# Second product of units 4 to 17 by seven block products alone, with forms made in fp32; the order of all work as one list

## The chip, the cores and the metric

The kernel runs on one NeuronCore of a Trainium2 chip. The metric is device time in microseconds (us) of one execution. The engines are TensorE (PE; PEld is its weight load), VectorE (DVE), ScalarE (ACT), GpSimd (POOL) and SyncE (SP), which issues most DMAs. Each engine works through its own list of instructions in order; semaphores hold one back until what it needs is done.

## The reference

```python
# q, k, v: (8, 8, 576, 64), phi: (8, 8, 576, 32), w_in: (512, 2048), w_out: (2048, 512)
a = softmax over the sequence of phi                      # 32 memory slots
k_m = einsum('bhsm,bhsd->bhmd', a, k);  v_m = the same with v
attn = softmax(q @ k_m.T / sqrt(64))
x = (attn @ v_m), heads side by side: 4608 tokens x 512
h = x @ w_in
g = h - tanh(h)
return g @ w_out                                          # 4608 x 512
```

The weights arrive as 64-bit floats.

## The kernel before

**Numbers.** Factors of the large products are pairs of fp16 tiles, high part and low part (`ah`/`al`, `win_hi`/`win_lo`, `wout_hi`/`wout_lo`, `gg[:, 0]`/`gg[:, 1]`). A product is the sum of high by high, high by low and low by high, all into fp32 PSUM. The 64-bit weights are turned into fp32 by three integer operations on DVE (`to_f32`), rounded to fp16 on ACT (`conv`), and their low halves formed on DVE, POOL or PE (`low`, `low_pool`, `low_pe`).

**Tiling.** The 4608 tokens are 18 units of 256, the 2048 hidden features four groups `fb` of 512; a unit and a group make a block, 72 blocks in all. For each of the 8 batches the attention gives `ah`/`al`, and `att_p` multiplies the memory's values with `w_in`, so that the first product `mm1` (word `H`) goes straight from attention weights to hidden values `hp` in PSUM.

**A block.** `mm1` ends with the square of `hp` on ACT (`uu`). The cubic for h - tanh(h) is `g1` on DVE (L576, one PSUM and one SBUF tile in), `g1_square` on ACT (L581), `g2` on DVE (L586, two SBUF tiles in from unit 4 on), giving the fp32 tile `h3` of 128 x 1024. `g2_high` rounds it to fp16 on ACT (L592), `g3` subtracts on POOL for the low part (L597). The second product adds the block into the unit's sums `o0` and `o1` (128 tokens x 512 each), in PSUM until the unit's last block.

**The second product.** In units 0 to 3 it is plain, `mm2` (L640). From unit 4 on it is `mm2_blocks`: the high by high part is plain, 8 matmuls of 512 columns (`main`, L697); the two cross terms go by seven products of blocks in place of eight (a scheme of Strassen's kind), 7 x 4 matmuls of 256 columns (L704). The seven need sums and differences ("forms") of four blocks of `g`, made by `a_forms` on DVE (L610) from the fp16 halves, and forms of `w_out`, made once from its fp16 halves by `b_form` (L622). Four of the seven add up in a PSUM tile `x` shared by all units; `evict` (L757 to L769) joins `x` with `o0`, `o1` on DVE and sends the unit out.

**The order.** Up to the third block of unit 4 it is the word list `START`, one word a step of one piece of work (`H10` the first product of unit 1, group 0; `T` and `L` weight conversion; `Z` a pair of filler matmuls). From there a loop over blocks writes the rest by the tables `PLAN`, `PLAN3`, `PLAN_C`: first product, `g1`, the square, `a_forms` of the block before, `g2`, the second product of two blocks back, rounding, `g3`. `in_order` fixes each engine's order as written.

```python
        g1(u, fb)
        do(0)
        g1_square(u, fb)
        a_forms(*forms.pop())
        g2(u, fb)
        queue.append((u, fb))
        v, vb = queue.pop(0)
        mm2_blocks(v, vb, vb == 0, vb == NFB - 1)
        do(1)
        g2_high(u, fb)
        g3(u, fb, nc.gpsimd)
```

Of the kernel before, what the change touches and what calls it, by code (L numbers as in the profile page):

```python
# [1138 lines left out]
```

## Time and profile before

| | |
|---|---|
| median of 3 runs | 663.79 us (661.35 to 664.32) |
| the profiled execution | 663.12 us, its span 661.3 us |
| mean granted TensorE clock | 0.997 |
| POOL, low part of `g` (L597) | 67 of 2.17 us |
| DVE, forms of `g` (L610) | 224, 0.43 to 0.49 us mean |
| DVE, cubic (L576, L586) | 144 of 1.22 us |

A profile row of a group reads: line, engine, operation, out<-in by the program's names, shapes, count | busy us, mean ns of one | idle time of that engine just before them, and what ended it. A row of waits reads: who <- what it waited for: us in total, times, longest. A timeline row reads: start, length, engine, what it was.

### The profile page before, as it was taken

The page shows a single profiled execution, that of the slowest core. Times are in us where ns is not written, and L with a number is a line of the kernel's source. Part 1 is how long each engine was busy: PE and PEld are TensorE (multiplying, and loading weights), DVE is VectorE, ACT ScalarE, POOL GpSimd, SP SyncE. Part 2 cuts the span into 40 slices and gives each one's busy share as a digit, 9 for nine tenths or more (in the row PEclk, how much of TensorE's full clock was granted, in tenths as well). Part 3 has the DMA queues.
Part 4 walks back from the last instruction along what each step waited for, and adds up shares of the span by engine and source line. Part 5 has one row for each costly group of instructions (what it writes and reads, how often), then busy time and mean ns, then how long its engine had stood idle before and what let it go on. Part 6 is the DMA issues. An engine that isn't in the chain of part 4 may idle for free.

```text
span 661.3 us, 15304 instructions
## 1 busy us (share of the span) xinstructions
PE 635.6 (96%) x6562; PEld 452.1 (68%) x6562; DVE 539.1 (82%) x840; ACT 352.1 (53%) x445; POOL 222.7 (34%) x141
## 2 busy tenths in 40 slices
PE   8678999999999999999999999999999999899996
PEld 4254656555657777777777777777786767677885
DVE  6798999999846797875888789778977897979573
ACT  4576576665523555545555555555555546554441
POOL 0224331443112234451435243633362423332321
PEclk9998999999999999999999999999999999999999
DMA  8999253333122301324231433143314432224101
GB/s 341 400 361 384 64 196 105 126 99 113 65 96 101 135 30 73 113 100 145 93 113 66 167 105 113 66 168 103 115 47 152 140 119 65 97 96 160 34 33 37
DMA packets 25995, 84.96 MB, mean 128 GB/s; under 512 B 2880, under 2 KB 2880, under 8 KB 25152
## 3 DMA queue, kind: packets, MB, share of 16 engines
q1 hardware_dynamic: 24624, 81.55, 34.7%
q10 hardware_dynamic: 1296, 2.36, 0.9%
q8 instruction: 53, 0.87, 0.5%
q14 instruction: 22, 0.18, 0.1%
HBM read 72.37 MB, written 11.53 MB: 127 GB/s over the span
## 4 chain that ended last, share of the span: by engine, by line
PE 61%; DVE 23%; DMA 5%; issue 4%; ACT 4%; POOL 2%; SPq 0%; DVEq 0%; ACTq 0%; POOLq 0%
PE hs L561 16%; PE x L704 11%; PE o L697 11%; PE o L704 8%; PE o L640 5%; DMA raw<-in_w_out_dram 3%; DVE h L586 3%; DVE h L576 3%; PE h L561 2%; DVE f L610 2%; DVE wt L387 2%; PE pp L513 2%; DVE ph L531 2%; PE pkv L223 2%; PE o1h L640 2%
## 5 line engine op out<-in xcount | busy, mean ns | idle before, releaser
L597 POOL TENSOR_TENSOR g<-h,g 128x1024 f16<-128x1024 f32 x67 | 145.7, 2174 | 357.1 <-ACT g L592 294.3
L561 PEld LDWEIGHTS <-ph 128*128 128x128 f16 x2304 | 177.7, 98 | 22.2 <-issue 6.6
L561 PE MATMUL hs<-ah,ph 128*128 128x256 f16 (+3 forms) x1152 | 151.5, 246 | 0.0
L592 ACT ACTIVATE g<-h 128x1024 f16<-128x1024 f32 x72 | 76.0, 1056 | 113.5 <-DVE h L586 105.0
L576 DVE SCALAR_TENSOR_TENSOR h<-hs,u 128x1024 f32<-128x1024 f32 x54 | 65.7, 1217 | 77.2 <-ACT u L568 76.9
L561 PE MATMUL hs<-al,ph 128*128 128x256 f16 (+3 forms) x576 | 127.6, 246 | 0.3 <-POOL al L504 0.3
L581 ACT ACTIVATE u<-u,beta 128x1024 f32<-128x1024 f32 x72 | 82.5, 1148 | 61.0 <-DVE h L576 60.6
L697 PE MATMUL o<-wout_hi,g 128*128 128x512 f16 x432 | 104.7, 379 | 2.3 <-DVE r L769 2.3
L704 PEld LDWEIGHTS <-f 128*128 128x128 f16 x896 | 87.7, 98 | 10.2
L586 DVE SCALAR_TENSOR_TENSOR h<-u,h 128x1024 f32<-128x1024 f32 x72 | 87.6, 1216 | 0.7 <-ACT u L581 0.7
L568 ACT ACTIVATE u<-hs 128x1024 f32<-128x1024 f32 x54 | 55.0, 1019 | 59.4 <-PE hs L561 55.3
L704 PEld LDWEIGHTS <-g 128*128 128x128 f16 x672 | 64.2, 98 | 28.7 <-issue 7.3
L704 PE MATMUL x<-bt,f 128*128 128x256 f16 x672 | 82.5, 273 | 0.0
L697 PEld LDWEIGHTS <-g 128*128 128x128 f16 x432 | 40.6, 98 | 46.5 <-issue 10.8
L640 PEld LDWEIGHTS <-g 128*128 128x128 f16 x384 | 36.7, 98 | 46.6 <-issue 4.3
L640 PE MATMUL o<-wout_hi,g 128*128 128x512 f16 x192 | 59.0, 379 | 0.0
L610 DVE TENSOR_TENSOR f<-g 128x512 f16<-128x512 f16 x112 | 50.7, 493 | 4.0 <-POOL g L597 3.4
L561 PE MATMUL h<-ah,ph 128*128 128x256 f16 (+3 forms) x384 | 50.7, 248 | 1.1 <-DVE h L576 1.1
L561 PE MATMUL h<-al,ph 128*128 128x256 f16 (+2 forms) x192 | 42.9, 248 | 0.1
L531 DVE SCALAR_TENSOR_TENSOR ph<-pp,ph 128x1024 f16<-128x1024 f32 x31 | 37.7, 1215 | 0.7 <-ACT ph L526 0.3
L526 ACT ACTIVATE ph<-pp 128x1024 f16<-128x1024 f32 x32 | 32.5, 1017 | 7.6 <-PE pp L513 7.5
L640 PE MATMUL o<-wout_lo,g 128*128 128x512 f16 x96 | 36.4, 379 | 0.0
(146 smaller groups left out, 934.2 us busy)
## 6 DMA issues: line engine op xcount, KB each, us to landing
kv<-in_kva_dram SPq DMA_DIRECT2D x20, 516.0 KB, 3.9
q<-in_qt_dram SPq DMA_DIRECT2D x16, 576.0 KB, 4.2
chk<-in_w_in_dram SPq DMA_DIRECT2D x16, 512.0 KB, 5.2
chk<-in_w_out_dram SPq DMA_DIRECT2D x16, 512.0 KB, 3.7
out_dram<-r SPq DMA_DIRECT2D x27, 256.0 KB, 2.3
kv<-in_kva_dram SPq DMA_DIRECT2D x6, 1032.0 KB, 9.7
raws<-in_w_in_dram SPq DMA_DIRECT2D x12, 512.0 KB, 8.0
raw<-in_w_out_dram SPq DMA_DIRECT2D x12, 512.0 KB, 8.9
```

The source lines that it names most:

```text
L531: nc.vector.scalar_tensor_tensor(pl, pa, S_P / (S_V * S_W), ph, op0=ALU.mult, op1=ALU.subtract)
L561: nc.tensor.matmul(hp[:, k, tu : tu + w], px[:, g, cs], d[ax][:, g, ta : ta + w], start=(n == 0), stop=(n == 5),)
L568: nc.scalar.activation(uu, hp, AF.Square, scale=1.0 / (S_A * S_P))
L576: nc.vector.scalar_tensor_tensor(h3, hp, C2 * S_G / (S_A * S_P), uu, op0=ALU.mult, op1=ALU.mult)
L581: nc.scalar.activation(uu, uu, AF.Square, bias=c["beta"])
L586: nc.vector.scalar_tensor_tensor(h3, uu, CC, hp, op0=ALU.add, op1=ALU.mult)
L592: nc.scalar.activation(gg[:, 0], h3, AF.Copy)
L597: eng.tensor_tensor(gg[:, 1], h3, gg[:, 0], op=ALU.subtract)
L610: nc.vector.tensor_tensor(o, x, y, op=op)
L640: nc.tensor.matmul(o, gx[:, k, P * tt : P * tt + P], wx[:, 4 * fb + k, :], start=(first and k == 0 and wx is wout_hi and gx is gh), stop=( ...
L697: nc.tensor.matmul(o[th], gg[:, 0, k, P * th : P * th + P], wout_hi[:, 4 * fb + k, :], start=(first and k == 0), stop=False)
L704: nc.tensor.matmul(dst, a(1 - n, kk), b(n, kk), start=(new and kk == 0 and n == 0), stop=(end and kk == 1 and n == 1))
```

## The change

1. In units 4 to 17 the plain part is gone: each of the seven products has all three terms, 7 x 6 matmuls of 256 columns (`mm2_blocks`).
2. The forms of `g` are made from the fp32 tile `h3` (`s_forms`, four DVE operations on 128 x 256 fp32) and then split: the high half by one ACT operation of 128 x 1024, the low half by one POOL operation of 128 x 1024 (`s_high`).
3. Of `g` itself three of its four blocks are split, by two ACT and two POOL operations (512 and 256 elements; `a_high`, `a_low`).
4. The forms of `w_out` are made from an fp32 sum of its halves and split in the same way (`b_sum`, `b_form` on DVE, `b_high` on ACT, `b_low` on POOL), per group.
5. The weight conversion works on 1024 elements where it worked on two times 512; pairs of raw weight blocks come in one DMA.
6. `START`, the tables and the loop are replaced by one list, `ORDER`, in which a word stands once for each step of its piece; a second product has three to five steps, an eviction six. The DMA scratch is 1024 bytes.

```diff
+ORDER = """
+i3:pp5 i1:gg i0:gg T0 T0 FX0 Z0.0 Z0.0 Z0.0 Z0.0 X0 T0 i6:kv3 T3 T3 T3 i4:kv2 Z0.0 Z0.0 Z0.0 Z0.0 Z0.0 Z0.0 Z0.0 Z0.0 Z0.0 Z0.0 Z0.0 T2 T2 Z0.0 T2
...
-        for r, t in zip(r32, ts):
-            nc.vector.scalar_tensor_tensor(
-                t, r[:, :, 0], 29, t, op0=ALU.logical_shift_right, op1=ALU.bitwise_or
-            )
+        for low, high, t in parts:
+            nc.vector.scalar_tensor_tensor(t, low, 29, t, op0=ALU.logical_shift_right, op1=ALU.bitwise_or)
...
-        eng.tensor_tensor(gg[:, 1], h3, gg[:, 0], op=ALU.subtract)
+    def a_parts(u, fb):
+
+        h3, gg = hs[u, fb], gs[u, fb]
+        if (u, fb) not in SEVEN:
+            return ((h3, [gg[:, n] for n in range(2)]),)
+        return (
+            (h3[:, 2:4], [gg[:, n, 2:4] for n in range(2)]),
+            (a_block(h3, 0, 0), [a_block(gg[:, n], 0, 0) for n in range(2)]),
+        )
+
+    def a_high(u, fb):
+        gs[u, fb] = big.tile([P, 2, 4, UT], F16, tag="gg", name=f"g{u}{fb}", bufs=3)
+        for x, (hi, _) in a_parts(u, fb):
+            nc.scalar.activation(hi, x, AF.Copy)
+
+    def a_low(u, fb, eng):
+        for x, (hi, lo) in a_parts(u, fb):
+            eng.tensor_tensor(lo, x, hi, op=ALU.subtract)
...
-        gg = gs[u, fb][1]
-        a11, a21, a12, a22 = (a_block(gg, th, kh) for kh in range(2) for th in range(2))
-        f = big.tile([P, 2, 4, 2, P], F16, tag="uu", name=f"f{u}{fb}")
-        s4, s3, s1, s2 = (f[:, :, i] for i in range(4))
+        h3 = hs[u, fb]
+        a11, a21, a12, a22 = (a_block(h3, th, kh) for kh in range(2) for th in range(2))
+        s = big.tile([P, 4, 2, P], F32, tag="ss", name=f"s{u}{fb}")
+        s1, s2, s3, s4 = (s[:, i] for i in range(4))
         for o, x, y, op in ((s3, a21, a11, ALU.subtract), (s1, a21, a22, ALU.add), (s2, s3, a22, ALU.add), (s4, a12, s2, ALU.subtract)):
             nc.vector.tensor_tensor(o, x, y, op=op)
+    def s_high(u, fb):
+
+        s = fs[u, fb]
+        f = big.tile([P, 2, 4, 2, P], F16, tag="uu", name=f"f{u}{fb}")
+        nc.scalar.activation(f[:, 0], s, AF.Copy)
+        yield
+        nc.gpsimd.tensor_tensor(f[:, 1], s, f[:, 0], op=ALU.subtract)
+        fs[u, fb] = f
...
+    def b_sum(fb):
+
+        bts["w", fb] = b = big.tile([P, 4, 512], F32, tag="bw", name=f"bw{fb}", bufs=1)
+        ks = slice(4 * fb, 4 * fb + 4)
+        nc.vector.tensor_tensor(b, wout_hi[:, ks], wout_lo[:, ks], op=ALU.add)
+
+    def b_form(fb):
+
+        b = bts["w", fb]
+        b11, b12, b21, b22 = (b[:, 2 * kh : 2 * kh + 2, 256 * nh : 256 * nh + 256] for kh in range(2) for nh in range(2))
+        for o, x, y in ((b11, b12, b11), (b12, b12, b22), (b22, b22, b11), (b21, b21, b22)):
+            nc.vector.tensor_tensor(o, x, y, op=ALU.subtract)
...
         def prod(dst, a, b, new=False, end=False):
             for kk in range(2):
-                for n in range(2):
+                for na, nb in ((0, 0), (0, 1), (1, 0)):
                     nc.tensor.matmul(
-                        dst, a(1 - n, kk), b(n, kk), start=(new and kk == 0 and n == 0), stop=(end and kk == 1 and n == 1)
+                        dst, a(na, kk), b(nb, kk), start=(new and kk == 0 and na == 0 and nb == 0), stop=(end and kk == 1 and na == 1)
                     )
...
+        prod(x[:, 0, hi], af(1), bf(0, 0), new=xfirst)
+        prod(x[:, 0, lo], ab(0, 0), bb(0, 0), end=xlast)
+        yield
+        prod(x[:, 1, lo], af(2), bf(1, 1), new=xfirst)
+        prod(x[:, 1, hi], af(3), bf(0, 1), end=xlast)
...
+        prod(o[0][:, hi], af(4), bb(1, 1), new=first)
+        prod(o[0][:, lo], ab(0, 1), bb(1, 0), end=last)
+        yield
+        prod(o[1][:, lo], ab(1, 1), bf(1, 0), new=first, end=last)
```

Three places show what this makes of the engines' lists. The first is PE inside a second product of the steady part before: the end of the plain part on a tile `g` (both factors high), and the first cross products.

```order
L697 LDWEIGHTS g_4330
L697 MATMUL o_4281<-wout_hi,g_4330 128x512
L704 LDWEIGHTS g_4330
L704 MATMUL o_4280<-wout_hi,g_4330 128x256
L704 LDWEIGHTS g_4330
L704 MATMUL o_4280<-wout_lo,g_4330 128x256
```

And after, inside a second product: the end of the product of a form `f` with a form `bt` of the weights, and the start of the next, on `g` and `w_out` themselves.

```order
L761 LDWEIGHTS f_5365
L761 MATMUL x<-bt_2221,f_5365 128x256
L761 LDWEIGHTS g_5495
L761 MATMUL x<-wout_hi,g_5495 128x256
L761 LDWEIGHTS g_5495
L761 MATMUL x<-wout_lo,g_5495 128x256
```

No matmul of 512 columns is left in these units; all are of 256, each with a weight load of its own.

The second place is DVE in the steady part before: the cubic's two steps (`h`) with the forms `f` of the block before between them.

```order
L576 SCALAR_TENSOR_TENSOR h_3568<-hs,u_3566 128x1024
L610 TENSOR_TENSOR f_3573<-g_3515 128x2x256 x2
L610 TENSOR_TENSOR f_3573<-f_3573,g_3515 128x2x256
L610 TENSOR_TENSOR f_3573<-g_3515,f_3573 128x2x256
L586 SCALAR_TENSOR_TENSOR h_3568<-u_3566,h_3568 128x1024
```

After, in a like stretch (`s` are the fp32 forms, L630 and L642 the cubic's steps):

```order
L367 RECIPROCAL sz_4263<-sz_4263 128x18
L630 SCALAR_TENSOR_TENSOR h_4268<-hs,u_4261 128x1024
L642 SCALAR_TENSOR_TENSOR h_4268<-u_4261,h_4268 128x1024
L675 TENSOR_TENSOR s_4296<-h_4176 128x256 x2
L675 TENSOR_TENSOR s_4296<-s_4296,h_4176 128x256
L675 TENSOR_TENSOR s_4296<-h_4176,s_4296 128x256
L675 TENSOR_TENSOR s_4301<-h_4268 128x256 x2
```

The forms have moved from between the two steps to behind them, and the forms of two blocks can follow each other; what stands between the two steps differs from block to block.

The third place is POOL before: one low part of `g` a block, with the softmax steps (`sc`) and the low part of the attention weights (`al`) between.

```order
L597 TENSOR_TENSOR g_4016<-h_3958,g_4016 128x1024
L305 TENSOR_TENSOR sc_3969<-sc_3969,sm_4024 128x576
L597 TENSOR_TENSOR g_4111<-h_4053,g_4111 128x1024
L318 TENSOR_TENSOR sc_3969<-sc_3969,sz_4116 128x576
L597 TENSOR_TENSOR g_4206<-h_4147,g_4206 128x1024
```

After:

```order
L684 TENSOR_TENSOR f_4173<-s_4002,f_4173 128x1024
L356 TENSOR_TENSOR sc_3974<-sc_3974,sm_4090 128x576
L684 TENSOR_TENSOR f_4240<-s_4120,f_4240 128x1024
L666 TENSOR_TENSOR g_4125<-h_4092,g_4125 128x512
L666 TENSOR_TENSOR g_4125<-h_4092,g_4125 128x2x128
L369 TENSOR_TENSOR sc_3974<-sc_3974,sz_4263 128x576
```

A block now has three operations on POOL, the forms' low half and two of `g`.

More of the change, by code (lines that the diff above doesn't have):

```diff
@@ new lines, in b_low, with segment, sums @@
+    def b_low(fb):
+        for k in range(0, 4, 2):
+            ks = slice(k, k + 2)
+            nc.gpsimd.tensor_tensor(bts[fb][:, 1, ks], bts["w", fb][:, ks], bts[fb][:, 0, ks], op=ALU.subtract)
+    acc = {}
+    def segment(u, fb):
+        part = [f for f in ((0, 1), (2, 3)) if fb in f][0] if u in SPLIT else tuple(range(NFB))
+        return part, [f for f in part if (u, f) in SEVEN]
+    def sums(u):
+        acc[u] = [ps_o.tile([P, DM], F32, tag=f"o{i}", name=f"o{u}{i}") for i in range(2)]
@@ L628, in mm2 @@
+    def mm2(u, fb):
+        if (u, fb) in SEVEN:
+            yield from mm2_blocks(u, fb)
+            return
+        part, seven = segment(u, fb)
+        first, last = fb == part[0], fb == part[-1]
+        gg = gs[u, fb]
         gh, gl = gg[:, 0], gg[:, 1]
@@ L632, in mm2 @@
         elif first:
-            acc[u] = [ps_o.tile([P, DM], F32, tag=f"o{i}", name=f"o{u}{fb}{i}") for i in range(2)]
+            sums(u)
         both, less = ((wout_hi, gh), (wout_lo, gh)), ((wout_hi, gl),)
         order = [(0, both), (0, less), (1, both), (1, less)] if last else [(0, both), (1, both), (0, less), (1, less)]
-        for tt, part in order:
+        for n, (tt, terms) in enumerate(order):
+            if n == 2:
+                yield
             o = acc[u][tt]
             for k in range(4):
-                for wx, gx in part:
+                for wx, gx in terms:
                     nc.tensor.matmul(
@@ L815, in split_path, with go @@
+        "T": conv, "L": low_pool, "Lv": low, "Lp": low_pe,
+        "BS": b_sum, "BF": b_form, "BH": b_high, "BL": b_low,
+        "SI": squares_in, "NI": norms_in, "SO": squares_out, "NO": norms_out, "SS": squares_sum, "CW": window,
+        "GG": lambda: check(tc, c, big), "GX": lambda: check_all(tc, c, ps_a), "XX": steady, "WD": flag,
+        "M": mm2, "E": evict, "R": load_part, "OP": save_part, "O": save,
     }
     going = {}
-    def go(word, whole=True):
-        name = word.rstrip("0123456789")
-        run = going.pop(word, None) or STEPS[name](*(int(x) for x in word[len(name):]))
-        if run is None or not hasattr(run, "send"):
+    def go(word):
+        if ":" in word:
+            k, tag = word.split(":")
+            n = int(k[1:])
+            if k[0] == "k":
+                load_raw(n, tag, "chk")
+            elif tag in PAIRS:
+                load_raws(n + 16 * (k[0] == "o"), tag)
+            else:
+                load_raw(n + 16 * (k[0] == "o"), tag)
@@ L917, in split_path @@
-    a_forms(*forms.pop())
-    for u, fb in queue:
-        mm2_blocks(u, fb, fb == 0, fb == NFB - 1)
-    c["wide"] = nc.values_load(c["bad"][0:1, 0:1], min_val=0, max_val=1)
-    evict()
+    for word in ORDER.split():
+        go(word)
     in_order(tc, c["first"])
@@ L1000, in wide_path @@
         att.top_all(b, d)
-        list(att.expo(b, d))
+        att.expo(b, d)
+        att.expo_exp(b, d)
         att.pool(b, d)
```

464 lines of the change are left out of this document (200 added, 264 removed), and 12 rows, old and new, of tables (PLAN, PLAN3, PLAN_C).

## The prediction

> **What bounds the kernel now.** I read the page first, then busy time by stretches, the waits, the timeline of one steady block and the groups by form.
>
> ```profile
> span 661.3 us, 15304 instructions
> PE 635.6 (96%) x6562; PEld 452.1 (68%) x6562; DVE 539.1 (82%) x840; ACT 352.1 (53%) x445; POOL 222.7 (34%) x141
> ```
>
> The profiled execution took 663.1 us, 0.7 under the median of the runs (663.8); 1.8 us lie outside its span. PE is busy for 96%, but the stages differ:
>
> ```profile
> core 0: us, PE busy (x) PEld busy (x) DVE busy (x) ACT busy (x) POOL busy (x), PEclk, DMA share, GB/s
> 0.00:20.00 20.00, 17.12 (x92) 7.91 (x92) 15.00 (x30) 9.81 (x16) 0.95 (x10) 1.00 0.92 354
> 20.00:40.00 20.00, 14.06 (x195) 6.51 (x196) 14.93 (x32) 10.72 (x20) 7.63 (x7) 1.00 0.97 377
> 40.00:60.00 20.00, 15.77 (x205) 11.53 (x204) 18.78 (x30) 15.90 (x27) 3.19 (x3) 0.91 1.00 397
> 100.00:120.00 20.00, 20.00 (x227) 11.66 (x226) 19.93 (x32) 13.28 (x22) 4.42 (x3) 1.00 0.46 162
> 180.00:200.00 20.00, 20.00 (x157) 11.21 (x156) 10.57 (x15) 4.26 (x5) 3.47 (x2) 1.00 0.24 80
> 260.00:320.00 60.00, 59.69 (x622) 45.69 (x621) 44.59 (x73) 30.71 (x39) 22.17 (x13) 1.00 0.31 104
> 380.00:440.00 60.00, 60.00 (x701) 45.55 (x700) 50.22 (x80) 32.67 (x41) 24.45 (x15) 1.00 0.34 114
> 560.00:620.00 60.00, 56.16 (x537) 44.13 (x535) 51.02 (x78) 30.04 (x33) 19.15 (x10) 1.00 0.30 106
> ```
>
> Up to 60 us DMA is 92 to 100% busy and PE is idle for 13 us; around 100 us PE and DVE are both full; from 180 us on PE alone is full or nearly so, DVE is idle for 15 to 47% and POOL for over half. So the steady part is paid in PE time, and what DVE loses there is free until its reserve is gone. That reserve is its wait for the square of the next first product:
>
> ```profile
> DVE h L576 <- ACT u L568: 78.6, 41, 3.6
> PE psc L275 <- DVE vl L487: 3.7, 2, 2.5
> PE o L697 <- DVE r L769: 2.3, 3, 1.1
> PE x L704 <- DVE r L758: 1.8, 2, 1.5
> L576 DVE SCALAR_TENSOR_TENSOR h<-hs,u x54: 1160/1224/1226, 198.2 to 642.9; 128x1024 f32<-128x1024 f32 x54
> ```
>
> The last row (a line's durations, min/median/max in ns, and its first and last start) gives the steady period: (642.9 - 198.2) / 53 = 8.39 us a block. The reserve is 78.6 / 54 = 1.46 us of it. PE's own longest waits are few and already are for DVE (the values' low half, the eviction of a unit).
>
> **The change, part by part.**
>
> *PE.* The pitch of its two forms:
>
> ```profile
> 400.30 1.89 PE L697 MATMUL o<-wout_hi,g 128*128 128x512 f16 x8
> 402.03 0.27 PE L704 MATMUL o<-wout_hi,g 128*128 128x256 f16 x1
> 409.87 1.47 PE L704 MATMUL x<-bt,f 128*128 128x256 f16 x12
> 411.18 0.27 PE L704 MATMUL o<-wout_hi,f 128*128 128x256 f16 x1
> ```
>
> From start to start: (402.03 - 400.30) / 8 = 0.216 us for 512 columns, (411.18 - 409.87) / 12 = 0.109 for 256. A block's second product was 8 x 0.216 + 28 x 0.109 = 4.78 us; it becomes 7 x 6 = 42 x 0.109 = 4.58. That is 0.20 us less for each of 56 blocks: **-11.3 us**, all on the path while PE bounds, and a steady period of 8.19. The six added weight loads a block stand beside matmuls as the others do. Of the rest of PE's work (first product, attention, units 0 to 3) nothing is dropped or added.
>
> *DVE, ACT, POOL in a steady block.* Prices:
>
> ```profile
> L610 DVE TENSOR_TENSOR f<-g 128x512 f16<-128x512 f16 x112 | 50.7, 493 | 4.0 <-POOL g L597 3.4
> L610 DVE TENSOR_TENSOR f<-g x112: 380/417/1623, 184.9 to 650.4; 128x512 f16<-128x512 f16 x112
> L762 DVE TENSOR_TENSOR r<-r x14: 409/418/420, 229.4 to 655.7; 128x256 f32<-128x256 f32 x14
> L586 DVE SCALAR_TENSOR_TENSOR h<-u,h x72: 1182/1218/1225, 45.6 to 645.5; 128x1024 f32<-128x1024 f32 x72
> L417 DVE SCALAR_TENSOR_TENSOR wout_lo<-wt,wout_hi x10: 680/684/2614, 48.0 to 142.5; 128x512 f16<-128x512 f32 x10
> L769 DVE SCALAR_TENSOR_TENSOR r<-o,r x27: 672/681/691, 229.7 to 655.1; 128x512 f32<-128x512 f32 x27
> L592 ACT ACTIVATE g<-h 128x1024 f16<-128x1024 f32 x72 | 76.0, 1056 | 113.5 <-DVE h L586 105.0 <-PE o L640 5.2 <-DVE stat L475 1.6
> L404 ACT ACTIVATE wout_hi<-wt x16: 612/630/635, 27.4 to 138.7; 128x512 f16<-128x512 f32 x16
> L742 ACT ACTIVATE r<-x x14: 362/364/383, 226.9 to 653.1; 128x256 f32<-128x256 f32 x14
> L597 POOL TENSOR_TENSOR g<-h,g x67: 2120/2133/3008, 49.2 to 647.9; 128x1024 f16<-128x1024 f32 x67
> L436 POOL TENSOR_TENSOR wout_lo<-wt,wout_hi x4: 1159/1160/2148, 65.7 to 103.7; 128x512 f16<-128x512 f32 x4
> L168 POOL TENSOR_TENSOR e<-e,ms x8: 521/577/641, 283.8 to 488.5; 64x128 f32<-64x128 f32 x8
> ```
>
> DVE's four forms on 512 fp16 elements (0.417 each) become four on 256 fp32 elements (0.418): nothing. ACT's rounding of 1024 (1.056) becomes 512 + 256 + the forms' 1024, 0.63 + 0.36 + 1.06 = 2.05: +1.0 us a block on an engine with nearly 4 us of idle in it, so free. POOL's 2.13 becomes 1.16 + x + 2.13, where x (256 elements) lies between the 128-element row (0.58) and the 512-element one (1.16); nearer the first, 0.65: 3.94 a block, +1.8, or +101 us in all, a share of about 50%.
>
> *DVE and POOL do not run side by side.* The row of L610 says so: 1.62 us at most against 0.42. One such place:
>
> ```profile
> 281.47 2.37 POOL L162 TENSOR_TENSOR e<-e,ms 128x1024 f32<-128x1024 f32 x1
> 282.75 1.96 DVE L610 TENSOR_TENSOR f<-g 128x512 f16<-128x512 f16 x2
> 283.78 1.24 POOL L168 TENSOR_TENSOR e<-e,ms 64x128 f32<-64x128 f32 x2
> 284.63 0.67 DVE L610 TENSOR_TENSOR f<-f,g 128x512 f16<-128x512 f16 x1
> ```
>
> Two forms that need 0.83 us take 1.96, since POOL holds on to 283.84, and the third ends at 285.30, 0.28 after POOL's last. L417, another kind of operation with two SBUF tiles, waited up to 2.61 as well. After, the two steps of a block that read two SBUF tiles (the cubic's second product, L586, and the forms) meet a POOL queue of three operations a block instead of one. Ledger of a block: POOL 3.94, plus the attention's share (the 60 us from 260 on: 22.2 less 7.15 blocks x 2.13, over 7.15: 0.97; from 380 on 1.29; take 1.1); DVE 1.22 + 4 x 0.42, and 0.2 for the eviction: 3.1. Sum 8.1 of 8.19 us. That is gross: a waiting operation of 0.42 needs 0.28 once POOL is done, and two POOL operations of 512 take 0.19 more than one of 1024, so some 0.14 and 0.19 of each can pass beside the other: 5 x 0.14 + 3.8 x 0.19 = 1.4 off, 6.7 of 8.19, 82% (before: 6.3 gross of 8.39). It fits, without much room.
>
> The row of L586 itself shows no wait (1.225 at most): if it were outside, the ledger would be 8.1 - 1.2 = 6.9 gross. I count it, by L417. The Trainium skill, "GPSIMD Engine Reference", section 8 (Key points), says that GpSimd shares its SBUF interfaces with VectorE and contends with instructions in a two-port mode or with two SBUF inputs. By that L586 collides too, which is the side that speaks against the change; L610 and L417 agree with it, and no row here has a steady L586 meet POOL.
>
> What collisions cost DVE: at least nothing (each falls into a pause); at most two POOL operations of 2.13 a block, one before each of the two steps, 4.3. The nearest row is L610 itself: a mean of 493 against a median of 417 is 8.5 us over its 112, 0.15 a block, with POOL 37 to 41% busy; with POOL at (3.94 + 1.1) / 8.19 = 62%, four fp32 forms and a second step that meets it I take 0.5. Against DVE's reserve stand also the pauses between the cubic's two products: in the order before the forms filled them; after, in ten of the last 54 blocks nothing stands between, and ACT's square (1.15) plus the handover is waited for; with the shorter gaps counted, 0.3 us a block over all. Reserve left: 1.46 - 0.20 - 0.3 - 0.5 = 0.46 us a block. So the steady part stays PE's on the mean; single late pieces will still reach PE at unit ends, as the evictions do now. I allow **+2 us** (0 to 8).
>
> *Forms of the weights.* Eight fp16 operations of 1.22 (9.7 us) become four sums of 2048 fp32 elements, 2.28 each (twice L586 less its fixed 0.15), and sixteen of 512 (0.68): 20 us, +10 on DVE. In the order only the first sum stands in the stretch where DVE is full; the others are spread from unit 4 to early unit 5, against 9.4 us of idle DVE in 180 to 200 alone. **0**, at most +10 with that cover gone.
>
> *The opening.* The same 52 filler matmuls, the same bytes in 8 fewer DMA issues, DVE some 5 us less (24 conversions and 9 low halves of the weights in one operation for two, 0.15 of fixed time each). PE's 13 idle us to 60 us come from chains that were reordered; no row prices the new order. Between half of them saved and as much added: -6 to +6; I take **0**.
>
> *The end.* The last unit's half row leaves by one operation of 256 instead of two:
>
> ```profile
> 656.59 0.41 DVE L766 SCALAR_TENSOR_TENSOR r<-o,r 128x256 f32<-128x256 f32 x1
> 657.04 0.38 ACTq L767 DMA_DIRECT2D out_dram<-r  x1
> ```
>
> **-0.4**. Sum: 663.1 - 11.3 + 2 - 0.4 = 653.4, say 653.
>
> **The rivals.**
>
> *DVE with POOL becomes the bound: slower.* A wait takes the reserve's place. For it: the gross ledger of 99%, and queues that cannot be passed: a form held behind POOL also holds the next block's first cubic step, on which the tile of the next first product hangs. Against it: 82% net, and POOL's work is needed two blocks later. Its point: the reserve before collisions is 0.96 us a block, so PE starts to lose beyond that, and the gain of 0.20 is eaten at 1.16. At 1.4 us a block (two thirds of a POOL operation before each step) the cost is 0.44 x 54 = 24 us: 663.1 - 11.3 + 24 = 676.
>
> *The gain goes in the transition and at unit ends: no change.* For it: DVE full around 100 us; the ten more us of weight forms if they come there; 14 evictions, five of which cost PE 4.1 us already. Price +10: 662.
>
> *The new opening is tighter as well: much faster.* Half of the 13 us: 646 or less. Nothing in the rows asks for it.
>
> **How the numbers follow.** Forecast (PE bound, 646 to 659) 0.58; collisions bound (667 to 690) 0.20; gain used up (659 to 667) 0.14; tighter opening (under 646) 0.08. Below 645 lie some 0.07, above 672 some 0.13: range 645 to 672. Half a per cent, 3.3 us, is about what a measurement here can tell from no change (the runs span 661.4 to 664.3). Faster (under 660.5): 0.58 + 0.08 + a little of the third, 0.68; same 0.13; slower 0.19.
>
> **What would show it.** Right: the steady period of the cubic's first step near 8.2 us, PE over 97% from 200 us on, POOL near 50% of the span, forms at 0.42 median with a longer tail. The collisions' rival: PE idle before the first product with DVE's first cubic step as releaser, forms whose mean is near 1 us. The third: PE waits on evictions or a later start of the steady part than 195 to 200 us. The forecast is wrong if PE falls under 94% after 200 us, or if the first 60 us shift by over 6.

## The result, and the profile after

The changed kernel takes 672.98 us (median of 4 runs, 671.2 to 673.4), the kernel before 662.57 in the same comparison: a ratio of 1.0152, 95% interval 1.0114 to 1.0189. It is slower by 10 us, where I forecast 653 and a range of 645 to 672. Medians and ratios leave out the few executions in which the granted clock was near 0.6 throughout (one of e8_best below, two of the kernel before).

The first lines of the page, and some stretches, both of the changed kernel:

```profile
span 670.9 us, 16165 instructions
PE 633.5 (94%) x6882; PEld 485.1 (72%) x6882; DVE 584.8 (87%) x818; ACT 402.4 (60%) x541; POOL 371.5 (55%) x257
```

```profile
core 0: us, PE busy (x) PEld busy (x) DVE busy (x) ACT busy (x) POOL busy (x), PEclk, DMA share, GB/s
0.00:20.00 20.00, 18.30 (x66) 7.78 (x67) 9.85 (x15) 5.76 (x6) 0.96 (x10) 1.00 0.91 344
20.00:40.00 20.00, 14.01 (x178) 6.47 (x176) 17.73 (x34) 9.42 (x13) 6.72 (x5) 0.66 0.80 314
200.00:260.00 60.00, 55.27 (x618) 42.77 (x617) 54.15 (x69) 33.96 (x47) 42.65 (x27) 1.00 0.25 85
260.00:320.00 60.00, 58.62 (x693) 50.47 (x691) 53.88 (x79) 37.10 (x56) 39.42 (x28) 1.00 0.38 124
320.00:380.00 60.00, 59.87 (x664) 49.94 (x663) 54.38 (x73) 38.09 (x48) 42.87 (x30) 1.00 0.24 83
380.00:440.00 60.00, 55.29 (x632) 45.60 (x631) 48.01 (x71) 35.11 (x55) 35.53 (x26) 0.97 0.32 111
```

The stretches tell three places apart. In the opening DVE does 9.85 us of work in the first 20 us (15.00 before), and the granted clock is 0.66 from 20 to 40 us (1.00 before). From 200 to 260 us PE is busy for 55.3 of 60 us, from 380 to 440 for 55.3 (60.0 before), with POOL at 36 to 43 us of 60 where it had 20 to 24. From 320 to 380 us PE is full: there the change does what it should. (The kernel before, from 200 to 260 us: PE 59.8, DVE 44.6, POOL 19.7.)

Of the waits of DVE and of PE, some of the longest (in total, times, longest):

```profile
DVE h L642 <- ACT u L632: 19.5, 16, 3.1
DVE h L630 <- ACT u L616: 10.2, 15, 1.5
...
DVE h L630 <- POOL g L666: 3.5, 3, 1.7
```

```profile
PE pp L560 <- DVE ph L578: 6.0, 3, 2.6
...
PE hs L609 <- DVE h L630: 2.0, 4, 0.9
```

DVE's reserve, its wait for the square ahead of the first cubic step (now L630), fell from 78.6 us to 10.2. PE now waits for DVE in many places, 0.3 to 2.6 us each. By line, out<-in, shapes, count | busy us, mean ns | idle before:

```profile
L642 DVE SCALAR_TENSOR_TENSOR h<-u,h 128x1024 f32<-128x1024 f32 x72 | 98.5, 1369 | 19.8 <-ACT u L632 19.5
L630 DVE SCALAR_TENSOR_TENSOR h<-hs,u 128x1024 f32<-128x1024 f32 x54 | 65.6, 1214 | 13.8 <-ACT u L616 9.9 <-POOL g L666 3.5
L675 DVE TENSOR_TENSOR s<-h 128x256 f32<-128x256 f32 x112 | 59.5, 571 | 1.8
L675 DVE TENSOR_TENSOR s<-h,s 128x256 f32<-128x256 f32 x56 | 32.8, 585 | 1.9
L806 DVE TENSOR_TENSOR r<-r 128x256 f32<-128x256 f32 x14 | 12.9, 918 | 0.0
L630 DVE SCALAR_TENSOR_TENSOR h<-hs,u x54: 1160/1217/1226, 194.5 to 646.6; 128x1024 f32<-128x1024 f32 x54
```

The forms (L675) have the median I gave them (0.418 us), but means of 0.57 and 0.585; the second cubic step (L642) a mean of 1.369 against 1.216 before. The first cubic step (L630), which reads the product in PSUM, is untouched: a mean of 1.214, and by the last row (shortest, median, longest, first and last start) never over 1.226. That row also gives the period: (646.6 - 194.5) / 53 = 8.53 us a block, where I expected 8.2 and the kernel before has 8.39.

To lay the runs side by side I read two numbers from each trace: when the first product of block (1,0) starts (the opening's end), and how long it is from there to the end of the span. Before: 40.8 and 620.5 us. Changed: 46.7 and 624.2. So 5.9 us of the 9.6 are lost in the opening. From there on 3.7 are lost although PE's work should be 11.3 us less, so 15.0 go elsewhere. Most of that is waiting: after 60 us PE is idle for 610.9 - 586.0 = 24.9 us, before for 601.3 - 588.7 = 12.6. Each trace is one execution, and executions of one kernel differ by some us (the eight of e3_nolowf below lie between 664.2 and 669.8). So a difference of 1 to 3 us between two traces shows where time went, but not surely what an edit is worth.

### The profile page after: what moved, and what is told of

Its sections match the earlier page's. It is cut to its first block, busy times and chain, and to the rows that moved or that the text cites. A ratio compares the mean times of both kernels' runs of the same rounds, so it can differ in the third digit from the quotient of the medians.

```text
span 670.9 us, 16165 instructions
## 1 busy us (share of the span) xinstructions
PE 633.5 (94%) x6882; PEld 485.1 (72%) x6882; DVE 584.8 (87%) x818; ACT 402.4 (60%) x541; POOL 371.5 (55%) x257
## 5 line engine op out<-in xcount | busy, mean ns | idle before, releaser
L666 POOL TENSOR_TENSOR g<-h,g 128x256 f16<-128x256 f32 (+1 forms) x123 | 149.0, 1232 | 111.0 <-ACT g L662 106.6
L684 POOL TENSOR_TENSOR f<-s,f 128x1024 f16<-128x1024 f32 x56 | 125.7, 2245 | 84.1 <-ACT f L682 65.6
L761 PEld LDWEIGHTS <-f 128*128 128x128 f16 x1344 | 128.8, 98 | 31.4 <-issue 12.1
L761 PE MATMUL x<-bt,f 128*128 128x256 f16 x1008 | 128.4, 273 | 4.4 <-DVE r L802 2.0
L642 DVE SCALAR_TENSOR_TENSOR h<-u,h 128x1024 f32<-128x1024 f32 x72 | 98.5, 1369 | 19.8 <-ACT u L632 19.5
L616 ACT ACTIVATE u<-hs 128x1024 f32<-128x1024 f32 x54 | 55.1, 1020 | 52.9 <-PE hs L609 31.2
L662 ACT ACTIVATE g<-h 128x512 f16<-128x512 f32 (+2 forms) x128 | 68.4, 580 | 23.6 <-DVE h L642 19.7
L630 DVE SCALAR_TENSOR_TENSOR h<-hs,u 128x1024 f32<-128x1024 f32 x54 | 65.6, 1214 | 13.8 <-ACT u L616 9.9
L682 ACT ACTIVATE f<-s 128x1024 f16<-128x1024 f32 x56 | 58.8, 1050 | 25.5 <-DVE s L675 19.8
L675 DVE TENSOR_TENSOR s<-h 128x256 f32<-128x256 f32 x112 | 59.5, 571 | 1.8
L742 PE MATMUL o<-wout_hi,g 128*128 128x512 f16 x192 | 59.0, 379 | 2.2 <-ACT g L662 2.2
L761 PE MATMUL o<-wout_hi,f 128*128 128x256 f16 x224 | 46.5, 275 | 1.2 <-DVE r L811 1.2
L761 PE MATMUL o<-wout_hi,g 128*128 128x256 f16 x224 | 46.5, 275 | 0.0
L761 PE MATMUL x<-wout_hi,g 128*128 128x256 f16 x224 | 45.9, 273 | 0.5 <-POOL g L666 0.5
```

Source lines behind the costliest of these rows:

```text
L616: nc.scalar.activation(uu, hp, AF.Square, scale=1.0 / (S_A * S_P))
L630: nc.vector.scalar_tensor_tensor(h3, hp, C2 * S_G / (S_A * S_P), uu, op0=ALU.mult, op1=ALU.mult)
L642: nc.vector.scalar_tensor_tensor(h3, uu, CC, hp, op0=ALU.add, op1=ALU.mult)
L662: nc.scalar.activation(hi, x, AF.Copy)
L666: eng.tensor_tensor(lo, x, hi, op=ALU.subtract)
L675: nc.vector.tensor_tensor(o, x, y, op=op)
```

## The experiments

All are the changed kernel with the edit named, each timed against the kernel before. The ratio is to the kernel before, with its 95% interval; the last two columns are the two numbers just defined, from the one execution that was traced. The five kernels without low halves read a high half twice in their place: they do the same work on PE, but leave out the small part of the values that those halves carry.

| run | edit | median us | ratio | (1,0) starts | from there |
|---|---|---|---|---|---|
| (changed) | | 672.98 | 1.0152 (1.0114 to 1.0189) | 46.7 | 624.2 |
| e1_open | old opening | 669.43 | 1.0128 (1.0090 to 1.0167) | 40.7 | 626.7 |
| e2_fill | more fillers | 666.93 | 1.0085 (1.0066 to 1.0104) | 42.9 | 625.9 |
| e3_nolowf | no low halves of forms | 667.54 | 1.0078 (1.0046 to 1.0110) | 43.7 | 622.9 |
| e13_nolowg | no low halves of g | 669.81 | 1.0122 (1.0101 to 1.0143) | 46.7 | 621.3 |
| e14_nolowfg | neither of these two | 663.84 | 1.0046 (1.0029 to 1.0063) | 43.2 | 618.5 |
| e4_nolowb | no low halves of weight forms | 667.19 | 1.0070 (1.0043 to 1.0096) | 46.9 | 620.3 |
| e11_nopool | none of the three | 658.04 | 0.9951 (0.9931 to 0.9970) | 43.2 | 611.9 |
| e5_loop | old order | 723.31 | 1.0942 (1.0921 to 1.0964) | 40.1 | 678.9 |
| e6_e9 | eviction of unit 9 | 668.81 | 1.0091 (1.0062 to 1.0121) | 45.7 | 622.0 |
| e7_trans | three words, 225 to 245 us | 671.53 | 1.0132 (1.0102 to 1.0162) | 46.9 | 624.1 |
| e10_trans2 | five words there | 668.84 | 1.0114 (1.0083 to 1.0144) | 44.8 | 621.2 |
| e8_best | opening and moves | 667.32 | 1.0088 (1.0053 to 1.0123) | 40.2 | 624.5 |
| e9_best2 | other moves | 664.02 | 1.0042 (1.0016 to 1.0067) | 41.1 | 618.7 |
| e12_best3 | three moves more | 666.38 | 1.0078 (1.0048 to 1.0108) | 40.9 | 622.4 |

The intervals of e1_open, e13_nolowg, e6_e9, e7_trans, e10_trans2 and e8_best overlap that of the changed kernel. Their times alone do not tell them from it; what is said of them rests on their traces.

**The opening.**

```
 e1_open: the list up to the last filler in the order of START before
-i3:pp5 i1:gg i0:gg T0 T0 FX0 Z0.0 Z0.0 Z0.0 Z0.0 X0 T0 ...
+i0:gg i1:gg T0 Z0.0 Z0.0 Z0.0 T0 T0 T0 Z0.0 FX0 ...
 e2_fill: 12 words Z0.0 more, ahead of V0.0, V0.1, U0, Lp9, PLp0.0, P0.1
```

> The changed kernel with its list's words up to the last filler in the order of the kernel before (loads of raw weights i0, i1 first, fillers spread to 42 us); all later words as changed. Theory A (the change's loss is made of the opening, +6 us by the first block of unit 1, and of places after 200 us where VectorE and GpSimd hold each other up): the first conversion starts near 4.7 us instead of 8.5, the granted clock stays full from 20 to 40 us, unit 1 starts 5 to 6 us sooner, time 667 (664 to 669). Theory B (the opening's loss is taken up again by later waits, since VectorE is full around 100 us): unit 1 sooner, but the steady part starts within 2 us of where it did, time 671 to 673.

> The changed kernel with 12 filler words (24 matmuls of 512 columns) more, put between 21 and 42 us ahead of the TensorE pieces that wait there; nothing else is moved. Theory A: the half clock from 24.4 to 38.0 us comes from TensorE's pauses, and costs the opening about 2.5 us of its 6; with the fillers the granted clock is 1.0 from 20 to 45 us, matmuls of 512 fp32 columns stay near 0.43 us, and unit 1 starts 2 to 3 us sooner; time 670. Rival: TensorE only waits in the opening, so a half clock there costs nothing; unit 1 starts where it did (within 0.5 us) or later by the fillers themselves.

A row of the changed kernel's timeline (start, length, engine, what) and, of the stretches, the row from 20 to 40 us of e1_open and then of e2_fill:

```profile
8.51 0.76 DVE L438 TENSOR_SCALAR wt<-raw 128x512 uint32<-128x512 uint32 x2 [6.67 <-DMA raw<-in_w_in_dram]
```

```profile
20.00:40.00 20.00, 14.59 (x198) 6.71 (x197) 14.98 (x32) 10.97 (x18) 7.58 (x6) 1.00 0.96 367
```

```profile
20.00:40.00 20.00, 17.44 (x223) 7.33 (x222) 17.50 (x34) 11.12 (x16) 6.83 (x5) 0.91 0.85 326
```

This first conversion of weights waits for raw weights, and the new list asks for i3 first where the old one asks for i0 and i1. With the old opening it starts at 4.64 us, and block (1,0) at 40.7, 6 sooner, with the full clock, as theory A has it. But 1.9 us of that are lost again by block (0,1), 16 us later, and the time, 669.4, lies just above what theory A gave (664 to 669).

With fillers block (1,0) starts at 42.9 and the clock is 0.91 rather than 0.66. The time, 666.9, is better than the 670 expected; the traced execution is the slowest of its five (670.7).

Nine executions of the new opening as it is are in these traces. In the five with a granted clock of 0.66 block (1,0) starts at 45.7 to 46.9, in the four with 0.82 to 0.91 at 43.2 to 44.8; the mean is 45.3, 4.5 over before. So the opening is late by 2.4 us at least, and by 1 to 4 more where the clock is at 0.66. How much of the 2.4 is the late first conversion stays open, since e1_open changes the loads and the places of the fillers together. That the clock falls is not the fillers' absence alone, since it falls in some executions and not in others; what tips it stayed open too.

**Collisions of VectorE with GpSimd.**

```
 e3_nolowf
-        nc.gpsimd.tensor_tensor(f[:, 1], s, f[:, 0], op=ALU.subtract)
-            return lambda n, kk: f[:, n, i - 1, kk]
+            return lambda n, kk: f[:, 0, i - 1, kk]
 e13_nolowg: the same for a_low, e4_nolowb: for b_low; e14_nolowfg and e11_nopool: two and all three
```

> The changed kernel without GpSimd's low half of the forms of the left factor (56 operations of 2.24 us, 125 us of GpSimd); the products read the high half twice, so TensorE does the same number of matmuls. Theory A (collisions of VectorE with GpSimd are what the steady part pays): VectorE's forms fall from a mean of 0.57 us to under 0.47, the second cubic step from 1.37 to 1.25, and of the 15 us of TensorE stalls added after 200 us at least 8 go: time 660 to 665. Theory C (the stalls come from where the list puts the pieces on the in-order queues, not from GpSimd): the stalls at 206 to 246 and 410 to 430 us stay, under 4 us are won: 669 to 672.

> The changed kernel without the low halves of the weight forms on GpSimd (8 operations of 2.2 us between 165 and 240 us); the products read the high half twice, TensorE's work is the same. Theory A (collisions with these make the transition late): VectorE's weight forms fall to 0.75 us each, unit 6 starts 4 to 6 us sooner against unit 1 than in the changed kernel; time 666 to 669. Theory C (the order of the pieces): unit 6 starts at most 2 us sooner.

> The changed kernel, its order untouched, without any low half of units 4 to 17 on GpSimd: not of g, not of the forms, not of the weight forms (some 180 operations, about 240 us of GpSimd); the products read the high halves twice, TensorE's work is the same. What GpSimd still does is the attention's. Collision theory (each late piece starts with a VectorE operation that GpSimd holds up): VectorE's forms at 0.42 us on the mean, and of TensorE's pauses after 60 us (26 us, 8 of them there in the kernel before too) all but 9 to 13 go; the eviction of unit 9 still waits once; 657 to 662 us. Order theory (in-order queues wait for each other without any collision): under 5 us are won as without the forms' low halves alone; 665 to 669.

> The changed kernel, order untouched, without GpSimd's low halves of g in units 4 to 17 (112 operations, some 100 us of GpSimd); the products read the high half twice. If these carry the loss (they start while VectorE is in the forms or the second cubic step, and the tile of the cubic is free only when they end): from the first block of unit 1 on 6 to 9 us are won, 660 to 664 us. If no single kind carries it, and what one leaves free another fills (the forms' low halves alone won 0.4 us there): under 3 us, 667 to 671.

> The changed kernel without GpSimd's low halves of g and of the forms in units 4 to 17, those of the weight forms kept. With all three left out 11.3 us were won from unit 1 on, with the weight forms' alone 4, with the forms' alone 0.4. If the parts add up once the steady ones are both gone: 7 us from unit 1 on, 661 to 664. If the transition's 4 us need the weight forms' part alone and the rest is spread: unit 6 within 1.5 us of the changed kernel, then 6 to 8 us won in units 6 to 17.

e11_nopool, its page and the same groups (L626 and L614 are the second and first cubic step, L661 the forms, L791 an eviction step):

```profile
span 655.1 us, 15872 instructions
PE 626.7 (96%) x6882; PEld 484.0 (74%) x6882; DVE 529.7 (81%) x818; ACT 401.9 (61%) x541; POOL 108.3 (17%) x81
```

```profile
L626 DVE SCALAR_TENSOR_TENSOR h<-u,h 128x1024 f32<-128x1024 f32 x72 | 87.9, 1221 | 20.5 <-ACT u L616 20.3
L614 DVE SCALAR_TENSOR_TENSOR h<-hs,u 128x1024 f32<-128x1024 f32 x54 | 65.8, 1218 | 32.7 <-ACT u L600 32.5
L661 DVE TENSOR_TENSOR s<-h 128x256 f32<-128x256 f32 x112 | 47.4, 464 | 0.7
L661 DVE TENSOR_TENSOR s<-h,s 128x256 f32<-128x256 f32 x56 | 24.1, 430 | 1.9
L791 DVE TENSOR_TENSOR r<-r 128x256 f32<-128x256 f32 x14 | 6.3, 453 | 0.0
```

With the same 818 operations on DVE, it is busy for 529.7 us instead of 584.8: GpSimd's low halves cost DVE 55 us, 1.0 a block. From block (1,0) on the kernel is 12.3 us shorter than the changed one (11.3 by the start of block (17,2)), and 8.6 shorter than the kernel before; PE is idle for 14.5 us after 60 us instead of 24.9. The time, 658.0, lies where the collision theory put it (657 to 662), 0.5% under the kernel before.

Not all of the 12.3 need be operations held up: DVE also waited 3.5 us at L630 and 2.2 at L365 for POOL to be done with `g`, and PE 1.2 for POOL's low halves (L684 and L666), and these waits are gone as well. What each is worth was not separated. Nor is e11_nopool free of collisions, since the attention's operations stay on POOL. Its longest pause of PE after 60 us stands behind one:

```profile
266.12 1.28 POOL L535 TENSOR_TENSOR al<-af,ah 128x576 f16<-128x576 f32 x1 [15.58 <-ACT ah L533]
267.36 2.54 POOL L194 TENSOR_TENSOR e<-e,ms 128x1024 f32<-128x1024 f32 x1
266.36 3.82 DVE L661 TENSOR_TENSOR s<-h 128x256 f32<-128x256 f32 x2
273.92 0.82 PE L746 MATMUL x<-bt,f 128*128 128x256 f16 x6 [2.79 <-DVE r L787]
```

Two forms take 3.82 us while POOL is busy up to 269.9, and L787, the eviction's step that PE waits for, stands behind them in DVE's list.

Whether the parts add up depends on what is summed. In DVE's busy time they do: without the forms' low halves it falls by 26.7 us, without those of g by 23.6, without those of the weight forms by 4.7, together 55.0 of 55.1. From block (1,0) on, in one trace each, they are worth 1.3, 2.9 and 3.9 us, 8.1 of 12.3; by the ratios, which hold the opening's scatter too, 0.74, 0.30 and 0.82%, 1.86 of 2.01. So a gap is not shown. What is plain is that PE's loss does not follow DVE's: the weight forms' low halves take 4.7 us of DVE and cost about as much time, those of the forms take 26.7 and cost 1 to 5. When the forms' low halves are gone, the forms still take 0.517 on the mean: those of g meet them:

```profile
L659 DVE TENSOR_TENSOR s<-h 128x256 f32<-128x256 f32 x112 | 53.3, 517 | 0.7
L659 DVE TENSOR_TENSOR s<-h,s 128x256 f32<-128x256 f32 x56 | 32.2, 574 | 1.9
```

So no kind alone carries the loss, as the second expectation on e13_nolowg has it; that what one leaves free another fills is not borne out by DVE's busy time. Of the other expectations, e3_nolowf (667.5) fell between its two theories, e4_nolowb met theory A (667.2, unit 6 sooner by 4.1 us against unit 1), and e14_nolowfg (663.8) won 5.7 us of the 7. e13 and e14 also hold a wait of PE that the other runs lack (first product on the second cubic step, 3.4 us near 190 us), which may hide some of their gain; its reason is open.

**The order.**

```
 e5_loop: the list rebuilt from the old START, tables and slot of a block;
 f of the block before between a and a, s after M, then g c
```

> The new arithmetic in the old order: the changed kernel with its list rewritten as the kernel before issued its work (its opening, its tables and its fixed slot of a block; the forms of a block stand between the next block's two cubic steps, their rounding after the evicted second product, and the weight forms at the old places and in the first two slots). Theory A: the opening's 6 us come back, the collisions stay as the arithmetic is the same: 664 to 668. Theory C: the order alone carries the loss, and the arithmetic brings its 11 us: 651 to 658. A third way: the old order was cut for shorter GpSimd work, and the later form halves make TensorE wait each block: over 675.

Its first waits of PE (L745 is the second product, L668 the low half of the forms):

```profile
PE x L745 <- POOL f L668: 28.0, 20, 5.2
PE pp L544 <- DVE ph L562: 14.8, 2, 10.9
```

The third way came true. In the old slot the forms of a block are made while the next one is computed and are wanted one slot later, but now they still have to go through ACT and an operation of POOL (2.16 us on the mean there). The new list, which spreads this over more blocks, is worth 50 us to the new arithmetic. (The old tables were not tuned for it; that a list between the two does better is not excluded.)

**One late step.** DVE in the changed kernel, from its timeline:

```profile
408.34 0.77 DVE L374 STREAM_TRANSPOSE af<-sc 128x576 f32<-128x576 f32 x1
413.16 0.42 DVE L800 SCALAR_TENSOR_TENSOR r<-x,r 128x256 f32<-128x256 f32 x1 [4.05 <-ACT ph L573]
...
417.79 1.87 DVE L675 TENSOR_TENSOR s<-h 128x256 f32<-128x256 f32 x2
...
422.67 2.59 DVE L642 SCALAR_TENSOR_TENSOR h<-u,h 128x1024 f32<-128x1024 f32 x1 [2.22 <-ACT u L632]
425.19 1.21 DVE L578 SCALAR_TENSOR_TENSOR ph<-pp,ph 128x1024 f16<-128x1024 f32 x1
```

The trace names ACT, which had given the eviction its rows at 408.4. More likely it was PE: the first step of M10.0, ahead of this step in the list, writes the other half of the same PSUM tile, and its matmuls end at 413.1. In e6_e9 two words change place:

```
-... M9.3 XP6 YM6 H10.3 P5.1 H10.3 M10.0 E9 E9 M10.0 E9 ...
+... M9.3 E9 E9 XP6 YM6 H10.3 P5.1 H10.3 M10.0 M10.0 E9 ...
```

> The changed kernel with two words moved: the first two steps of unit 9's eviction (VectorE's reads of the x sum) stand before the first step of unit 10's second product instead of behind it. As it is, VectorE's first read waits for a semaphore of TensorE that the last of those 12 matmuls raises, idles 4.05 us, and all of VectorE's queue behind it comes late. Theory C (order): the stalls of TensorE at 412.8, 415.3 and 423.6 us (1.2, 1.0 and 2.7 us) and the half clock at 427 to 430 us (1.7 us) go together, from 430 us on all is 5 to 6.5 us sooner, time 666 to 668. Rival (VectorE is full there and the wait only shows where its work piles up): under 2 us, time 671 to 673.

There the eviction's step starts at 408.9 without a wait, so the wait was for that step of PE. By block (12,0) 4.2 us are won, and the half clock at 427 to 430 us is gone; 2.0 are lost again around 565 us, at a wait for DVE that the changed kernel has too, now with a half clock behind it. So 2.2 us are left at the end, under what was expected (the time is 668.8, for 666 to 668). In this trace the order did matter: same work, other place.

**The transition, 200 to 260 us.**

```
 e7_trans: PL3.0 ahead of f5.0; g5.0 c5.0 behind P3.1 and BL3
 e10_trans2: also the second E4 and the first a5.2 ahead of f5.1
```

> The changed kernel with three words moved at 225 to 245 us: the low half of the attention's product of batch 3, part 0, on VectorE goes before the forms of block (5,0); the rounding of g of block (5,0) on ACT and its low half on GpSimd go before the first eviction's rows instead of behind them. Nothing is taken off any engine. Theory C: the 2.4 us wait of TensorE at 230.5 us and the 2 us of small waits at 242 to 246 go; unit 6 starts 3.5 to 5 us sooner; time 668 to 670. Theory A (VectorE and GpSimd have too much to do between 200 and 245 us, in any order): the waits move to other places, unit 6 starts within 1.5 us of where it did.

> The changed kernel with the three words of the transition moved as in the run before that moved them alone, and two more: the second step of unit 4's eviction and the first cubic step of block (5,2), both on VectorE, go before the forms of block (5,1), which the trace of that run shows held up by GpSimd from 239.8 to 243.9 us with the eviction behind them and TensorE waiting 3.0 us for it. No engine's work changes. Theory C (what is lost at 225 to 245 us is lost by what stands behind a held-up operation): unit 6 starts 3.5 to 5 us sooner against the first block of unit 1 than in the changed kernel, 667 to 669 us. Theory A (the load of VectorE and GpSimd together is the bound there): the wait moves once more and unit 6 starts within 1.5 us of where it did: 670 to 672.

In e7_trans PE's wait moved on to the eviction of unit 4. DVE there:

```profile
239.78 2.09 DVE L659 TENSOR_TENSOR s<-h 128x256 f32<-128x256 f32 x2
241.79 1.37 DVE L659 TENSOR_TENSOR s<-s,h 128x256 f32<-128x256 f32 x1
243.19 0.77 DVE L659 TENSOR_TENSOR s<-h,s 128x256 f32<-128x256 f32 x1
243.89 0.41 DVE L786 SCALAR_TENSOR_TENSOR r<-x,r 128x256 f32<-128x256 f32 x1
```

Four forms that need 1.7 us take 4.1. Against unit 1, as the expectations measure it, unit 6 starts 0.9 us sooner in e7_trans and, with the eviction ahead of the forms, 1.3 in e10_trans2: both within the 1.5 of theory A. Without the low halves of the weight forms (e4_nolowb) it starts 4.1 sooner, with PE at 57.8 of 60 us (55.3). So this place looks set by load more than by order, though a better order than these two is not excluded.

**All mends together.**

```
 e8_best: old opening, e6_e9, e7_trans, moves in units 10 and 14
 e9_best2: old opening, e6_e9, e10_trans2, other moves in units 10 and 14
 e12_best3: e9_best2 and PL5.1 ahead of a10.3's last step, f5.0 and f14.3 behind a5.1 and a15.0
```

> The changed kernel with the opening of the kernel before (as in the first run above), the two moves of the eviction and the transition, and three more of the kind: the low half of the attention's product behind the first eviction step (unit 10) and ahead of a block's forms (unit 14), and the first cubic step of block (15,2) behind two eviction steps. Arithmetic and work of every engine are as changed. Theory C: the gains add up, 5 (eviction) + 4 (transition) + 3 (opening, as measured) + 2 = 14 us: 657 to 660, level with the kernel before or faster. Theory A: what is won at one place is lost to VectorE's load at the next: 664 to 669.

> The changed kernel with the old opening, the moved eviction of unit 9, the moves of the transition just named, and three places mended where TensorE waited over 1 us for VectorE (units 10 and 14: eviction steps ahead of the low half of an attention product or of a cubic step; unit 14: that low half ahead of a block's forms). Work of every engine as changed. Theory C: opening 3.5, eviction 4, transition 4, the other three 3: 14 of the changed kernel's time, 656 to 659 and faster than the kernel before. Theory A: without the transition's 4, 660 to 663, level with the kernel before.

> The second run of all mends, with three more places of one kind, each a VectorE piece that GpSimd held up with TensorE's next piece behind it: the low half of an attention product moved into VectorE's pause before the second cubic step of block (10,3); the forms of blocks (5,0) and (14,3) moved behind the first cubic step that TensorE waits for. Same work on every engine. If a held-up operation costs only what stands behind it, the pauses at 226, 415 and 555 us (1.9, 2.3 and 2.7 us) go with the half clock behind them: 655 to 659 us, faster than before by 0.4 to 0.9%. If the load decides, the pauses come back a block later: 661 to 664.

None beats the kernel before. e8_best (667.3) came out where the load theory put it. e9_best2, with every engine's work as changed, comes to 664.0, above both of its expectations (656 to 659, or 660 to 663 if the load decides): by the ratios 1.1% under the changed kernel, 0.4% over the one before. e12_best3 (666.4, expected 655 to 659 or 661 to 664) took the pause at 415 us away; of its other two moves one brought a longer pause (4.6 us near 230 us for 1.8), the other left one as long as it was (2.6 near 560 us for 2.7):

```profile
PE psc L310 <- DVE ph L562: 4.6, 1, 4.6
PE pno L500 <- DVE ph L562: 2.6, 1, 2.6
```

The forms of block (5,0), moved behind the cubic step, met POOL there as well: three of them took 5.0 us. The moves tried here mostly changed who is late.

## Why the prediction was wrong, point by point

- *PE: 11.3 us less.* Right. The pitch held: twelve matmuls of the changed kernel start within 332.46 - 331.15 = 1.31 us, 0.109 each, as priced.

```profile
331.15 1.47 PE L761 MATMUL o<-bt,g 128*128 128x256 f16 x12
332.46 0.82 PE L761 MATMUL x<-bt,f 128*128 128x256 f16 x6
```

- *Collisions: 0.5 us a block, reserve 0.46 left, +2 us (0 to 8).* This is the step that failed: PE lost 12.3 us from block (1,0) on to POOL's low halves (e11_nopool). The price was less wrong than what I made of it. The two that I priced, forms and second cubic step, lost 59.5 - 47.4, 32.8 - 24.1 and 98.5 - 87.9 us to the low halves, 31.4 in all, 0.56 a block. The other 24 us of DVE's 55.1 fell on operations that I had not counted, above all the evictions (L806: 0.92 for 0.42) and the scaling of the softmax sums; some of that the kernel before paid already. But DVE's reserve was not used up on the mean: L630 still waits for the square for 10.2 / 54 = 0.19 us a block (19.5 us at L642, the pause between the cubic's two steps that I had put at 0.3, came to 0.36). I let the mean reserve decide, and allowed 2 us for single late pieces at unit ends. The traces show single hold-ups with PE's next piece behind them: forms that took 2.4 us longer at 239.8 us in e7_trans, 3.0 longer at 266.4 in e11_nopool, and PE waited 3.0 and 2.8 us. What DVE has to spare in other blocks does not help there.
- *The ledger, 82% net.* A ledger of sums says whether the work fits, not whether each piece is in time. DVE's own pauses, behind the cubic and at unit ends, need not lie where they could take up a collision.
- *POOL near 50%.* It is 55%: 222.7 before, +101 as forecast, 17.5 of the weight forms' low halves, which I left out, and the rest operations of POOL that took longer: the 256-element half 0.876 on the mean (I had 0.65; the shortest took 0.66), the 512-element one 1.361 against 1.16.
- *Forms of the weights: 0, at most +10.* 3.9 us in the trace of e4_nolowb, which leaves their low halves out. I priced DVE's part and left out that their low halves keep POOL busy in the same 60 us. If it is theirs alone, it is part of the 12.3.
- *The opening: 0 (-6 to +6).* +2.4 to +6.1, 4.5 on the mean: at the edge of its bounds, and 5.9 in the traced execution, where I put nothing into the sum. The order in which the raw weights are asked for stands in the first line of the new list; the first conversion could have been followed from there.
- *The end: -0.4.* Nothing shows against it.

In sum, for the profiled execution: 661.3 - 11.3 + 5.9 (opening) + 12.3 (POOL's low halves, those of the weight forms among them) + 2.7 = 670.9. The 2.7 is what is left over; the late eviction of unit 9 and the attention's collisions fall into it, but it was not taken apart.

The first rival had the cause, and its 676 is only 3 us off, but that is luck: it holds no opening. Its rule is the same mean reserve, 0.96 us a block before PE starts to lose. At the 1.0 us a block that DVE lost, that rule gives 0.04 x 54 = 2 us; PE lost 12.3. Of its signs one came and one did not: PE waits for DVE's first cubic step (2.0 us in 4 places), but the forms' mean is 0.57, not near 1 us. My two signs of a wrong forecast did not show either: PE is at 95% after 200 us (448.5 of 470.9; I expected over 97, and called under 94 wrong), and the opening shifted by 5.9 (over 6). They were set too wide.

The rule I weighed (the Trainium skill, "GPSIMD Engine Reference", section 8, Key points: contention with VectorE's instructions in a two-port mode or with two SBUF inputs) agrees with the main rows here. The forms, the evictions' sums (L806) and the second cubic step, which I could not see before, read two SBUF tiles and lost time to POOL; the first cubic step reads one of its inputs from PSUM and did not. One row is silent: the second form (s<-s,h) has two SBUF inputs as well and a mean of 0.459 us with the low halves, 0.461 without.

## What to carry to other kernels

An engine with a reserve on the mean is not safe when another can hold it up for whole operations. Ask which of its operations can be held up, which of those have PE's next piece right behind them, and whether one hold-up there is longer than the lead that piece has. When several kinds of operations crowd one engine pair, leave all of them out once before looking for the guilty one: here that gave 2.0% of the time, clear of the scatter, where the three kinds alone gave 0.3 to 0.8%. And follow the first words of a rewritten order up to the first operation that needs them.

## What the runs showed of the hardware

The clock fell to half after a pause of PE of 2.55 us (423.9 to 426.45). The stretch that holds the pause, the half clock, and the stretch behind it, in the changed kernel:

```profile
423.50:427.00 3.50, 0.95 (x28) 0.36 (x26) 3.41 (x3) 1.02 (x1) 3.35 (x4) 1.00 0.31 116
427.00:430.50 3.50, 3.50 (x32) 2.33 (x17) 2.29 (x3) 2.76 (x3) 1.32 (x1) 0.52 0.46 169
430.50:434.00 3.50, 3.50 (x68) 3.31 (x70) 3.43 (x9) 1.48 (x4) 0.00 (x0) 0.99 0.01 2
```

So a wait of 2.55 us cost (1 - 0.52) x 3.5 = 1.7 us more. The length of a pause alone does not decide: the clock also fell to half in e6_e9 behind a pause of 2.33 us at 229.8, and behind two of 1.02 and 0.88 us close together at 560.6. It stayed at 1.00 behind 2.79 us in e11_nopool (271 us), behind 2.70 in e9_best2 (555 us), and behind the same two of 1.02 and 0.88 in the changed kernel (565.4 us). What else decides is open. The Trainium skill, "TensorE: Matmul & The Clock Gate", "HAM oscillation", warns of pauses over some 3.4 us; here shorter ones did it.

A tiny operation that reads one SBUF tile took longer with POOL's work as well: the 18-element scaling of the softmax sums.

```profile
L366 DVE TENSOR_SCALAR sz<-sz x16: 176/439/1333, 35.4 to 571.9; 128x18 f32<-128x18 f32 x16
```

Without the low halves (e11_nopool) its median is 0.177 us and its mean 0.232; in the kernel before, which has low halves of `g` on POOL, the mean is 0.578. The Trainium skill, "SBUF — State Buffer", "Who interferes with whom", lists this kind (a scalar operation that can enter a two-port mode) beside those with two SBUF inputs. The row agrees with that; whether this operation runs in such a mode no run here shows.
